# Block-sparse attention with a gated feed-forward block: the band mask by a transposition, block means copied by VectorE, and the scores of the next unit two head pairs at a time

## The chip, the cores and the metric

The kernel runs on one core of one Trainium2 chip. The metric is the device time of one execution in microseconds (us). A core has five engines, each with its own queue, in which instructions stand in order: TensorE (PE) multiplies matrices, VectorE (DVE) and ScalarE (ACT) work on tiles and read the results of PE out of PSUM, GpSimd (POOL) works on tiles and issues DMAs, SyncE (SP) issues DMAs. PSUM has eight banks of 128 x 512 float32 numbers in this kernel: four of the pool `ps_mm`, two of `ps_s`, and one each of `ps_o` and `ps_t`.

## The reference

The first part is attention over 4 batches and 8 heads, with 768 positions and 64 columns a head. Each query sees the keys fewer than 16 positions away, and beside them a summary of every block of 32 positions (the elementwise maximum of its keys, the mean of its values). The second part runs the joined heads through a gated feed-forward block.

```python
k_sum = k.reshape(B, H, nb, block, D).max(axis=3)
v_sum = v.reshape(B, H, nb, block, D).mean(axis=3)
scores_l = scale * np.matmul(q, k.transpose(0, 1, 3, 2))
mask_l = np.abs(pos[:, None] - pos[None, :]) < window
scores_s = scale * np.einsum('bhsd,bhnd->bhsn', q, k_sum) + np.log(block)
scores_l_m = np.where(mask_l, scores_l, -1000000000.0)
a = softmax(np.concatenate([scores_l_m, scores_s], axis=-1))
x = np.matmul(a, np.concatenate([v, v_sum], axis=2))     # heads joined: (3072, 512)
g = x @ w_gate
gelu = 0.5 * g * (1.0 + erf(g / sqrt(2)))
ffn_out = (gelu * (x @ w_val)) @ w_out
out = x + sigmoid(x @ w_res) * ffn_out
```

Here d_ff is 1536 and the model width 512. `softmax` stands for the exponential and the division of the original.

## The kernel before, in words

The work is cut into eight units (`NU`), each half a batch: 384 positions, six tiles of 64 queries, four pairs of heads (`hp`). For a tile of queries, `kW` holds 128 columns of keys: its own 64, 16 on the left and 16 on the right (the rims), 24 block maxima and 8 empty ones. `vext` holds the values in the same order on 128 partitions, the block means on partitions 96 to 127.

A unit goes through these steps:

- **s**, `s_step` and `s_mm`: for a head pair, twelve matmuls of 64 contraction rows (six tiles, two heads) into two banks, one for each head. ScalarE takes the exponential into `P`, and from unit 1 on VectorE multiplies `P` with the band mask `maskt` of zeros and ones (L301). In unit 0 PE adds an additive mask `mneg` of large negative numbers ahead of the scores (L281) and no product is needed.
- **ao**, `av_step`: for a head pair, twelve matmuls of `P` with `vext` into one bank; `av_end` divides by the sum, which is one more column, into `xn` (L339, L341).
- **xT**: `xn` is transposed, in unit 1 by PE and ScalarE (`xt_step`), later by DMAs from SP's queue (`xt_dma`).
- **g, vv**: twelve steps `fo_step`, each with four matmuls for the gate and four for the value; ScalarE takes the Gelu (L366) and VectorE multiplies into `gvT` (L367).
- **r**: `res_step`, four matmuls for each of three blocks of 128 positions (`sub`), and a tanh on ScalarE.
- **f**: `ffn_step`, twelve matmuls for each block into one bank of `ps_mm`; `end_step` works the output out on VectorE (L415, then L418) and SP writes it.

The steps s, ao and xT of unit n + 1 stand within the r and f steps of unit n. The function `first_out` writes out this order for unit 0, `mid_out` for units 1 to 6; unit 7 has `last_out`. The order is that of the code: nothing is scheduled anew (`manual_schedule`), so each engine's queue holds its instructions as they are written. A pool hands its banks out in turn, and whoever gets a bank waits until its last reader is done. `ps_mm` has four banks in turn for g, vv, r, f; `s_step` uses the two banks of `ps_s`; `av_step` uses `ps_o`, or `ps_t` where `other` is given.

Unit 0 starts with loads. GpSimd's queue issues all loads from DRAM, in this order: keys and queries of batch 0, its values, six pairs of pieces of `w_gate` and `w_val` with the second half of the queries (`q_sb[1]`) between them, `w_res`, the rims of the later tiles, `w_out` in three pieces, then keys and values of batch 1. An issue waits for the landing of the eighth load before it. The mask `maskt` is cut out of ones by four selections (L196) after the third pair of pieces. The block means of unit 0 are summed by PE (`vsum_mm`) and copied into `vblk`. Unit 0's own values use `vblk` apart (`av_first`); the tiles 6 to 11 get the means by two copies on GpSimd (`vsum_bc`, L274), behind the issues of `w_out`. `keep_warm` runs matmuls on zeros between steps that wait. The functions `own_keys(bgrp, 3)`, `kw_consts(1)`, `vext_consts(1)` and two memsets of `vsum` fill constants for later batches on VectorE; they stand behind the first two gate steps.

`s_pair` is `s_step` for unit 0 with two banks of `ps_mm` and two exponentials.

Of the kernel before, what the change touches and what calls it, by code (L numbers as in the profile page):

```python
# [15 lines left out]
def kernel(  # L16
# [22 lines left out]
    QT = 64  # L39
# [95 lines left out]
    with tc.manual_schedule():  # L135
# [46 lines left out]
        nc.vector.memset(maskt[:], 1.0)  # L182
# [5 lines left out]
        for c in range(6):  # L188
            sl = slice(c * 256, (c + 1) * 256)
            nc.gpsimd.dma_start(out=w_gate[:, :, sl], in_=wg_src[:, :, sl])  # L190
            nc.gpsimd.dma_start(out=w_val[:, :, sl], in_=wv_src[:, :, sl])  # L191
            if c == 2:
                for lo, hi, sign, base, fill in (
                        (0, QT, 1, WIN - 1, 0.0), (0, QT, -1, WIN - 1, 0.0),
                        (QT, BAND, -1, WIN - 1 - QT, 0.0), (QT, BAND, -1, WIN, 1.0)):
                    nc.gpsimd.affine_select(out=maskt[lo:hi], in_=maskt[lo:hi], compare_op=ALU.is_ge,  # L196
                                            fill=fill, base=base, pattern=[[-sign, QT]],
                                            channel_multiplier=sign)
            if c == 4:
                q_sb[1] = load_q(1, QJ)  # L200
# [92 lines left out]
        def s_step(u, hp, st):  # L293
            s = ps_s.tile([128, 2, 512], F32, tag="s", name="s")
            s_mm(u, hp, [s[:, hh, 0:TU] for hh in range(2)])
            P = ppool.tile([128, 2, HT, QT], BF16, tag="P", name="P")
            nc.scalar.activation(P.rearrange("p a t q -> p a (t q)"), s[:, :, 0:TU], AF.Exp,  # L297
                                 scale=scale, bias=bias_t[:])
# [5 lines left out]
        def s_pair(hp, st):  # L304
            s = [mm_tile("s") for _ in range(2)]
            s_mm(0, hp, [x[:, 0:TU] for x in s])
            P = ppool.tile([128, 2, HT, QT], BF16, tag="P", name="P")
            for hh in range(2):
                nc.scalar.activation(P[:, hh].rearrange("p t q -> p (t q)"), s[hh][:, 0:TU], AF.Exp,
                                     scale=scale, bias=bias_t[:])  # L310
            st["P", hp] = P

# [159 lines left out]
        s_pair(1, st)  # L472
# [6 lines left out]
        s_pair(3, st)  # L479
        vsum_mm(0, vs, 5, 8)  # L480
        keep_warm(2)
        vsum_mm(0, vs, 8, NT)
        keep_warm(2)
# [5 lines left out]
        for i in range(2, 4):  # L489
            vsum_bc(0, 3 * i, 3 * i + 3, nc.gpsimd)  # L490

# [33 lines left out]
        for i in range(2):  # L525
            nc.vector.memset(vsum[i][96:128, :], 0.0)
        own_keys(bgrp, 3)
        kw_consts(1)
        vext_consts(1)


        def first_out(u, st, gvT, nst):
            n = u + 1
            turn = dict(pool=ps_t, tag="t", copy=nc.scalar.copy)
# [24 lines left out]
            xt_step(n, 3, nst, **turn)  # L559
# [124 lines left out]
```

## Time and profile before

| what | us |
|---|---|
| median of 11 runs | 267.07 |
| lowest and highest run | 265.76, 268.00 |
| the profiled execution: its own time | 266.75 |
| its span (first to last instruction) | 265.0 |
| VectorE busy | 154.5 |
| ScalarE busy | 126.2 |
| GpSimd busy | 108.5 |

An engine's busy time is the time in which at least one of its instructions ran. A row of the timeline has the start, the time, the engine, the line, what is written and read, and how many instructions of one kind follow each other; the wait before them stands at its end. A group's row has the busy time and mean nanoseconds of one, then the idle time before and what ended it. A row of windows has, for each engine, its busy time and its instructions, then the granted clock of PE, the mean time of DMA packets and the rate in GB/s. The granted clock was 0.998 of full speed over the whole span.

### The profile page before, as it was taken

The numbers are of one execution on the slowest core, as the hardware profiler recorded it, in microseconds if no ns is written. First come the engines' busy times: TensorE is split into PE (matmuls) and PEld (weight loads), VectorE is DVE, ScalarE is ACT, GpSimd is POOL, SyncE is SP. The second block draws the span as 40 slices with busy tenths as digits, with TensorE's granted clock in tenths as the row PEclk, the third lists the DMA queues.
The fourth block names the chain that finished last, engine by engine and source line by source line (L and its number), as shares of the span: only waits on it lengthen the run. The fifth ranks groups of instructions, "written<-read, shape, count | busy, mean of one in ns | idle before, by whom it ended". The sixth has DMA issues, their size and how long they took to land.

```text
span 265.0 us, 5801 instructions
## 1 busy us (share of the span) xinstructions
PE 257.2 (97%) x2297; PEld 138.2 (52%) x2297; DVE 154.5 (58%) x341; ACT 126.2 (48%) x197; POOL 108.5 (41%) x148
## 2 busy tenths in 40 slices
PE   6999998999999999999999999999999999999993
PEld 2556554545654565445654565445644565456543
DVE  5945732499557544667757444768667544754424
ACT  5774356565382436533373437342473337343320
POOL 8898375293260987253520986252620000000000
PEclk9999999999999999999999999999999999999999
DMA  5999999999743999979903999969803400240002
GB/s 83 175 119 186 197 214 207 188 136 190 72 79 62 171 132 145 103 131 167 134 0 95 161 123 130 121 120 169 131 14 80 127 0 2 46 136 0 0 13 108
DMA packets 98155, 29.61 MB, mean 112 GB/s; under 512 B 83368, under 2 KB 94960, under 8 KB 98016
## 3 DMA queue, kind: packets, MB, share of 16 engines
q0 software_dynamic: 68400, 14.96, 67.0%
q1 hardware_dynamic: 29728, 14.29, 25.0%
q8 instruction: 18, 0.29, 0.5%
q14 instruction: 9, 0.07, 0.1%
HBM read 29.36 MB, written 6.29 MB: 135 GB/s over the span
## 4 chain that ended last, share of the span: by engine, by line
PE 80%; DMA 11%; POOL 5%; DVE 1%; issue 1%; ACT 1%; POOLq 0%
PE f L409 23%; PE g L361 21%; PE vv L361 21%; PE r L399 7%; DMA w_out<-in_moe_w_out_dram 4%; DMA w_gate<-in_moe_w_gate_dram 4%; PE ao L321 3%; PE s L288 3%; DMA q_sb<-in_q_dram 3%; POOL vext L103 1%; POOL w_val L191 1%; POOL w_gate L190 1%; PE f L433 1%; PE vs L262 1%; PE tp L213 1%
## 5 line engine op out<-in xcount | busy, mean ns | idle before, releaser
L367 DVE TENSOR_TENSOR gvT<-ge,vv 128x384 bf16<-128x384 f32 x96 | 52.6, 552 | 53.3 <-PE vv L361 49.0
L366 ACT ACTIVATE ge<-g 128x384 f32<-128x384 f32 x96 | 47.1, 491 | 72.4 <-DVE gvT L367 40.9
L361 PE MATMUL g<-xT,w_gate 128*128 128x384 bf16 x384 | 79.0, 326 | 0.3
L361 PE MATMUL vv<-xT,w_val 128*128 128x384 bf16 x384 | 78.7, 326 | 0.2 <-DVE gvT L367 0.2
L409 PE MATMUL f<-w_out,gvT 128*128 128x512 bf16 x276 | 67.7, 380 | 0.9 <-DMA w_out<-in_moe_w_out_dram 0.9
L361 PEld LDWEIGHTS <-w_val 128*128 128x128 bf16 x384 | 37.5, 98 | 25.4 <-issue 1.0
L361 PEld LDWEIGHTS <-w_gate 128*128 128x128 bf16 x384 | 36.7, 98 | 26.0 <-issue 1.8
L409 PEld LDWEIGHTS <-gvT 128*128 128x128 bf16 x276 | 24.8, 98 | 28.1 <-DMA w_out<-in_moe_w_out_dram 1.4
L103 POOL DMA_DIRECT2D vext<-in_v_dram x48 | 32.9, 724 | 12.1 <-DMA w_out<-in_moe_w_out_dram 4.7
L297 ACT ACTIVATE P<-s,bias_t 128x768 bf16<-128x768 f32 x30 | 27.0, 901 | 15.1 <-PE s L288 14.5
L274 POOL COPY vext<-vsum 32x1536 bf16<-32x1536 bf16 x12 | 17.1, 1464 | 24.1 <-DMA vsum<-vpart 24.1
L415 DVE SCALAR_TENSOR_TENSOR th<-th,f 128x512 f32<-128x512 f32 (+1 forms) x25 | 16.5, 660 | 17.5 <-PE f L409 17.2
L402 ACT ACTIVATE th<-r 128x512 f32<-128x512 f32 x24 | 14.2, 595 | 26.1 <-PE r L399 26.0
L301 DVE TENSOR_TENSOR P<-P,maskt 128x768 bf16<-128x768 bf16 x28 | 15.9, 569 | 18.2 <-ACT P L297 18.2
L399 PE MATMUL r<-w_res,xT 128*128 128x512 bf16 x96 | 24.2, 380 | 0.0
L341 DVE TENSOR_TENSOR xn<-ao,rz 128x384 bf16<-128x384 f32 x32 | 17.8, 557 | 1.1
L418 DVE SCALAR_TENSOR_TENSOR o<-th,xn 128x512 f32<-128x512 f32 (+1 forms) x25 | 16.8, 670 | 0.9
L117 POOL DMA_DIRECT2D k_nat<-in_k_dram x24 | 16.4, 749 | 0.2 <-issue 0.2
L123 POOL DMA_DIRECT2D q_nat<-in_q_dram x18 | 15.9, 918 | 0.7 <-issue 0.6
L220 DVE TENSOR_REDUCE ks<-kW 128x24 bf16<-128x768 bf16 x16 | 15.1, 944 | 0.2
L321 PEld LDWEIGHTS <-P 128*64 128x64 bf16 x336 | 7.5, 110 | 11.9 <-issue 5.9
L399 PEld LDWEIGHTS <-xT 128*128 128x128 bf16 x96 | 8.7, 98 | 9.0
(84 smaller groups left out, 171.2 us busy)
## 6 DMA issues: line engine op xcount, KB each, us to landing
out_dram<-o SPq DMA_DIRECT2D x23, 256.0 KB, 2.2
vext<-in_v_dram POOLq DMA_DIRECT2D x48, 64.0 KB, 6.5
q_nat<-in_q_dram POOLq DMA_DIRECT2D x18, 128.0 KB, 7.3
w_gate<-in_moe_w_gate_dram POOLq DMA_DIRECT2D x6, 256.0 KB, 8.1
w_val<-in_moe_w_val_dram POOLq DMA_DIRECT2D x6, 256.0 KB, 8.7
w_out<-in_moe_w_out_dram POOLq DMA_DIRECT2D x3, 512.0 KB, 11.8
k_nat<-in_k_dram POOLq DMA_DIRECT2D x24, 64.0 KB, 4.7
vext<-vext SPq DMA_DIRECT2D x6, 144.0 KB, 5.4
```

Of the source, the lines that this page charges most:

```text
L103: nc.gpsimd.dma_start(out=vext[b % 2][0:QT, t, :, 0:D], in_=v[b, :, t * QT:(t + 1) * QT, :].rearrange("h p d -> p h d"))
L117: nc.gpsimd.dma_start(out=k_nat[:, t].rearrange("p (h d) -> p h d", d=D), in_=k[b, :, t * QT:(t + 1) * QT, :].rearrange("h p d -> p h d"))
L274: eng.tensor_copy(vext[b % 2][96:128, lo:hi, :, 0:D], src)
L297: nc.scalar.activation(P.rearrange("p a t q -> p a (t q)"), s[:, :, 0:TU], AF.Exp, scale=scale, bias=bias_t[:])
L341: nc.vector.tensor_mul(xn, ao[:, :, :, 0:D], rz.to_broadcast([128, NSUB, 2, D]))
L361: nc.tensor.matmul(ps[:, 0:TU], w[:, ko, fo * 128:(fo + 1) * 128], st["xT"][:, ko, :], start=(ko == 0), stop=(ko == KO - 1), skip_group_ch ...
L366: nc.scalar.activation(ge[:], g[:, 0:TU], AF.Gelu)
L367: nc.vector.tensor_mul(gvT[:, fo, :], ge[:], vv[:, 0:TU])
L399: nc.tensor.matmul(r[:], st["xT"][:, ko, ss], w_res[:, ko, :], start=(ko == 0), stop=(ko == KO - 1))
L409: nc.tensor.matmul(st["f", sub][:], gvT[:, fo, ss], w_out[:, fo, :], start=(fo == 0), stop=(fo == FO - 1), skip_group_check=True)
L415: nc.vector.scalar_tensor_tensor(th[:, cs], th[:, cs], 1.0, f[:, 0:n], ALU.add, ALU.mult)
L418: nc.vector.scalar_tensor_tensor(o.rearrange("p (k d) -> p k d", d=128), th[:, cs].rearrange("p (k d) -> p k d", d=128), 0.5, x, ALU.mult, ...
```

## The change

There are five edits.

- In units 1 to 6 (`mid_out`) scores 0 and 1 stand together, value products 0 and 1 with scores 2 and 3 behind them, and value products 2 and 3 together. Scores 1 lie in the banks of `ps_t` and `ps_o` (`TO2`), scores 3 in two banks of `ps_mm` (`MM2`); both have two exponentials of 384 columns. The blocks of r and f move between them.
- In unit 0 (`first_out`) scores 0 and 1 stand together, and value products 0 and 1. The last transposition (`xt_step` 3) stands ahead of the last four f.
- The mask `maskt` is no longer selected by GpSimd from ones. PE transposes `mneg` into a bank, and VectorE compares it with -1. This stands in `unit0_extras`, behind gate step 2.
- The block means for tiles 6 to 11 are copied by VectorE, two tiles behind each of the gate steps 4 to 6. The constants for later batches are spread over steps 2 to 9.
- In unit 0 the sums of values (`vsum_mm`) run through without the four warming matmuls between and behind them, and the products with own values follow them.

```diff
-        nc.vector.memset(maskt[:], 1.0)
...
-            if c == 2:
-                for lo, hi, sign, base, fill in (
...
-                    nc.gpsimd.affine_select(out=maskt[lo:hi], in_=maskt[lo:hi], compare_op=ALU.is_ge,
...
-        def s_step(u, hp, st):
-            s = ps_s.tile([128, 2, 512], F32, tag="s", name="s")
-            s_mm(u, hp, [s[:, hh, 0:TU] for hh in range(2)])
+        def s_step(u, hp, st, banks=None):
+            if banks:
+                s = [p.tile([128, 512], F32, tag=tag, name="s") for p, tag in banks]
+            else:
+                s2 = ps_s.tile([128, 2, 512], F32, tag="s", name="s")
+                s = [s2[:, hh] for hh in range(2)]
+            s_mm(u, hp, [x[:, 0:TU] for x in s])
...
+            if banks:
+                for hh in range(2):
+                    nc.scalar.activation(P[:, hh].rearrange("p t q -> p (t q)"), s[hh][:, 0:TU], AF.Exp,
+                                         scale=scale, bias=bias_t[:])
...
+        MM2 = ((ps_mm, "mm"),) * 2
+        TO2 = ((ps_t, "t"), (ps_o, "ao"))
...
-        vsum_mm(0, vs, 5, 8)
-        keep_warm(2)
-        vsum_mm(0, vs, 8, NT)
-        keep_warm(2)
+        vsum_mm(0, vs, 5, NT)
...
-        for i in range(2, 4):
-            vsum_bc(0, 3 * i, 3 * i + 3, nc.gpsimd)
...
+        def unit0_extras(fo):
+            if fo == 2:
+                mt = ps_o.tile([128, 128], BF16, tag="ao", name="mt")
+                nc.tensor.transpose(mt[:], mneg[:], ident[:])
+                nc.vector.tensor_scalar(out=maskt[:], in0=mt[:, 0:QT], scalar1=-1.0, scalar2=None,
+                                        op0=ALU.is_ge)
+                own_keys(bgrp, 3)
+            elif fo == 3:
+                kw_consts(1)
+            elif fo < 7:
+                vsum_bc(0, 2 * fo - 2, 2 * fo, nc.vector)
+            elif fo == 7:
+                vext_consts(1)
+            elif fo < 10:
+                nc.vector.memset(vsum[fo - 8][96:128, :], 0.0)
 
         def first_out(u, st, gvT, nst):
...
             s_step(n, 0, nst)
+            s_step(n, 1, nst, TO2)
             res_step(st, 0)
             res_step(st, 1)
             ffn_step(st, gvT, 0, 0, 4)
+            av_step(n, 0, nst)
+            av_step(n, 1, nst, **other)
+            s_step(n, 2, nst)
             ffn_step(st, gvT, 1, 0, 4)
-            av_step(n, 0, nst)
-            s_step(n, 1, nst)
             res_step(st, 2)
             ffn_step(st, gvT, 2, 0, 4)
-            ffn_step(st, gvT, 0, 4, 8)
-            av_step(n, 1, nst)
-            s_step(n, 2, nst)
             xt_step(n, 0, nst, **turn)
-            ffn_step(st, gvT, 1, 4, 8)
-            ffn_step(st, gvT, 2, 4, 8)
             av_step(n, 2, nst)
             s_step(n, 3, nst)
+            ffn_step(st, gvT, 0, 4, 8)
+            ffn_step(st, gvT, 1, 4, 8)
             xt_step(n, 1, nst, **turn)
+            ffn_step(st, gvT, 2, 4, 8)
+            av_step(n, 3, nst)
+            xt_step(n, 2, nst, **turn)
             ffn_step(st, gvT, 0, 8, FO)
             end_step(u, st, 0)
             ffn_step(st, gvT, 1, 8, FO)
-            av_step(n, 3, nst)
-            xt_step(n, 2, nst, **turn)
+            xt_step(n, 3, nst, **turn)
             ffn_step(st, gvT, 2, 8, FO)
-            xt_step(n, 3, nst, **turn)
             end_step(u, st, 1)
             end_step(u, st, 2)
...
             s_step(n, 0, nst)
+            s_step(n, 1, nst, TO2)
             res_step(st, 0)
-            ffn_step(st, gvT, 0, 0, 2)
-            s_step(n, 1, nst)
-            ffn_step(st, gvT, 0, 2, 6)
+            res_step(st, 1)
+            ffn_step(st, gvT, 0, 0, 4)
             av_step(n, 0, nst)
             xt_dma(0, nst)
-            s_step(n, 2, nst)
-            ffn_step(st, gvT, 0, 6, 11)
             av_step(n, 1, nst, **other)
             xt_dma(1, nst)
-            s_step(n, 3, nst)
-            ffn_step(st, gvT, 0, 11, FO)
-            res_step(st, 1)
+            s_step(n, 2, nst)
+            s_step(n, 3, nst, MM2)
+            ffn_step(st, gvT, 0, 4, FO)
+            ffn_step(st, gvT, 1, 0, 3)
             av_step(n, 2, nst)
             xt_dma(2, nst)
-            ffn_step(st, gvT, 1, 0, 4)
             av_step(n, 3, nst, **other)
             xt_dma(3, nst)
             end_step(u, st, 0)
-            ffn_step(st, gvT, 1, 4, FO)
+            ffn_step(st, gvT, 1, 3, FO)
             res_step(st, 2)
             end_step(u, st, 1)
             ffn_step(st, gvT, 2, 0, FO)
```

How the queues change is shown at three places; behind the line stand the operation, what it writes and reads, and its shape. On VectorE, these are the rows of unit 1's output phase before, from the mask products of head pairs 0 and 1 to the first step of `end_step`:

```order
L301 TENSOR_TENSOR P<-P,maskt 128x768 x2
L339 RECIPROCAL rz<-ao 128x6
L341 TENSOR_TENSOR xn<-ao,rz 128x384
L301 TENSOR_TENSOR P<-P,maskt 128x768
L339 RECIPROCAL rz<-ao 128x6
L341 TENSOR_TENSOR xn<-ao,rz 128x384
L301 TENSOR_TENSOR P<-P,maskt 128x768
L339 RECIPROCAL rz<-ao 128x6
```

And these are the same rows now:

```order
L302 TENSOR_TENSOR P<-P,maskt 128x768 x2
L334 RECIPROCAL rz<-ao 128x6
L336 TENSOR_TENSOR xn<-ao,rz 128x384
L334 RECIPROCAL rz<-ao 128x6
L336 TENSOR_TENSOR xn<-ao,rz 128x384
L302 TENSOR_TENSOR P<-P,maskt 128x768 x2
L334 RECIPROCAL rz<-ao 128x6
```

The mask products of pairs 2 and 3 stood behind the division of pair 0 and of pair 1; now both stand behind that of pair 1. On ScalarE, the same phase before, from the last Gelu to the load of the table for the next:

```order
L366 ACTIVATE ge<-g 128x384 x12
L297 ACT_TABLE_LOAD
L297 ACTIVATE P<-s,bias_t 128x768
L402 ACTIVATE th<-r 128x512
L297 ACTIVATE P<-s,bias_t 128x768 x3
L402 ACTIVATE th<-r 128x512 x2
L366 ACT_TABLE_LOAD
```

And now:

```order
L361 ACTIVATE ge<-g 128x384 x12
L298 ACT_TABLE_LOAD
L298 ACTIVATE P<-s,bias_t 128x768
L295 ACTIVATE P<-s,bias_t 128x384 x2
L397 ACTIVATE th<-r 128x512 x2
L298 ACTIVATE P<-s,bias_t 128x768
L295 ACTIVATE P<-s,bias_t 128x384 x2
L397 ACTIVATE th<-r 128x512
L361 ACT_TABLE_LOAD
```

Two of the four wide exponentials are now two narrow ones each, and two tanh stand between the pairs. On GpSimd, the loads of the start before, from the last piece ahead of the mask:

```order
L191 DMA w_val<-in_moe_w_val_dram 128x4x256
L196 AFFINE_SELECT maskt<-maskt 64x64 x2
L196 AFFINE_SELECT maskt<-maskt 32x64 x2
L190 DMA w_gate<-in_moe_w_gate_dram 128x4x256
L191 DMA w_val<-in_moe_w_val_dram 128x4x256
```

And now:

```order
L190 DMA w_val<-in_moe_w_val_dram 128x4x256
L189 DMA w_gate<-in_moe_w_gate_dram 128x4x256
L190 DMA w_val<-in_moe_w_val_dram 128x4x256
L189 DMA w_gate<-in_moe_w_gate_dram 128x4x256
L190 DMA w_val<-in_moe_w_val_dram 128x4x256
```

The selections are gone, and the loads keep their order.

More of the change, by code (lines that the diff above doesn't have):

```diff
@@ L302, in s_step @@
             st["P", hp] = P
[L304 to L311, printed above, removed]
+        MM2 = ((ps_mm, "mm"),) * 2
+        TO2 = ((ps_t, "t"), (ps_o, "ao"))
         def av_step(u, hp, st, pool=ps_o, tag="ao"):
@@ L524 @@
         gv_end(gvT, 1, g1, v1)
[L525 to L529, printed above, removed]
+        def unit0_extras(fo):
[13 more added lines that the diff above has]
+                nc.vector.memset(vsum[fo - 8][96:128, :], 0.0)
         def first_out(u, st, gvT, nst):
             n = u + 1
+            other = dict(pool=ps_t, tag="t")
             turn = dict(pool=ps_t, tag="t", copy=nc.scalar.copy)
             s_step(n, 0, nst)
+            s_step(n, 1, nst, TO2)
             res_step(st, 0)
@@ L619 @@
                     fo_step(st, gvT, fo)
+                if u == 0:
+                    unit0_extras(fo)
                 if u == 0 and fo >= 8:
```

13 lines of the change are left out of this document (5 added, 8 removed).

## The prediction

> **What bounds the kernel now.** I read the share of each engine on the page first, then the chain that ended last, then TensorE's own waits, and only then its timeline in one unit.
>
> ```profile
> PE 257.2 (97%) x2297; PEld 138.2 (52%) x2297; DVE 154.5 (58%) x341; ACT 126.2 (48%) x197; POOL 108.5 (41%) x148
> ```
> ```profile
> PE 80%; DMA 11%; POOL 5%; DVE 1%; issue 1%; ACT 1%; POOLq 0%
> ```
> ```profile
> PE xp L346 <- DVE xn L341: 0.2, 1, 0.2
> ```
>
> TensorE (PE) is 97% busy and carries 80% of the chain. The third row is the whole answer of the waits of PE between 56 and 248 us: once, for 0.2 us. So in units 1 to 6 nothing holds PE up from outside, and time can only leave there if PE's own stream gets shorter. A busy share of 97% does not say that the stream is as short as it can be, since the page counts the end of each matmul, which is pipelined, as busy. The places where the starts stand further apart than the work needs must be looked for in the timeline. This is unit 1's output phase, with one row per run of equal matmuls:
>
> ```profile
> 75.11 0.35 PE L288 MATMUL s<-qT,kW 64*128 64x64 bf16 x12
> 75.39 1.04 PE L399 MATMUL r<-w_res,xT 128*128 128x512 bf16 x4
> ```
> ```profile
> 77.07 1.04 PE L409 MATMUL f<-w_out,gvT 128*128 128x512 bf16 x4
> 78.04 0.38 PE L321 MATMUL ao<-vext,P 128*64 128x65 bf16 x12
> 78.35 0.35 PE L288 MATMUL s<-qT,kW 64*128 64x64 bf16 x12
> 78.63 1.25 PE L409 MATMUL f<-w_out,gvT 128*128 128x512 bf16 x5
> ```
> ```profile
> 85.78 2.75 PE L409 MATMUL f<-w_out,gvT 128*128 128x512 bf16 x12
> 88.37 0.65 PE L361 MATMUL g<-xT,w_gate 128*128 128x384 bf16 x3
> ```
>
> Starts count here. Twelve f from 85.78 to 88.37 take 2.59, or 0.216 each, so the four f from 77.07 need 0.86, but the value product (ao) starts 0.97 later: **0.10 us lost on the way into it**. For the way out I asked for narrow windows, in which the last two matmuls of a group stand alone:
>
> ```profile
> 75.26 0.19 PE L288 MATMUL s<-qT,kW 64*128 64x64 bf16 x2
> ```
>
> The score group (s) starts at 75.11 and its sixth pair at 75.26, so a pair takes 0.03. The residual product r follows at 75.39, 0.13 after that pair: **again 0.10 lost**. So a group of twelve costs 0.18 us of work and 0.10 wherever the shape of the tile in the third last column (64*128, 128*64, 128*128) changes.
>
> The other bound lies at the front. Up to 43.88 us the chain is not PE's:
>
> ```profile
> 32.67 11.16 DMA w_out<-in_moe_w_out_dram
> ```
> ```profile
> 43.88 1.90 PE L409 MATMUL f<-w_out,gvT 128*128 128x512 bf16 x8 [0.90 <-DMA w_out<-in_moe_w_out_dram]
> ```
>
> The first third of w_out is issued at 32.67 and lands 11.16 us later, at 43.83; PE, which stood still for 0.90 us, starts f on it.
>
> **Part 1: the order of unit 1 to 6's output phase.** Counted in the code's order, the old phase changes shape 14 times: into s, s to r, f to s, s to f, f to ao, ao to s, s to f, the last three once more, then r to ao, ao to f, f to ao, ao to f. The new one (scores 0 and 1 together, value products 0 and 1 with scores 2 and 3 behind them, value products 2 and 3 together) changes 7 times. The number of s, ao, r and f matmuls is the same. Seven changes at 0.10 are 0.70 us a unit.
>
> What two joined groups cost is shown for value products by one row only, and for scores by none:
>
> ```profile
> 16.89 0.61 PE L441 MATMUL wp<-warm 128*128 128x512 bf16 x2
> 17.43 1.04 PE L254 MATMUL vs<-vext,bmat 64*32 64x256 bf16 x8
> 18.40 0.60 PE L441 MATMUL wp<-warm 128*128 128x512 bf16 x2
> 18.94 0.95 PE L333 MATMUL ao<-vext,P 96*64 96x65 bf16 x48
> ```
>
> Four groups of twelve in a run keep PE busy for 0.95 here, 0.24 each against 0.31 from start to start for a single one. The join of two scores may cost from 0 to 0.10 on each side, thus 0.30 to 0.70 saved a unit. I take 0.70, because the pairs inside a group already follow each other at 0.03. The Trainium skill, "TensorEngine Tiling (Array Packing)", Tiling Modes, says that a change of the tiling mode drains the engine, and a change of the tile alone does not. By that rule joins are free and the saving is 0.70; without it, by the entries alone, it would be 0.30.
>
> What can now be late. Scores 1 and 3 lie in two separate banks, so ScalarE takes two exponentials of 384 columns instead of one of 768:
>
> ```profile
> 75.72 0.90 ACT L297 ACTIVATE P<-s,bias_t 128x768 bf16<-128x768 f32 x1
> 76.52 0.59 ACT L402 ACTIVATE th<-r 128x512 f32<-128x512 f32 x1
> ```
> ```profile
> 13.97 1.07 ACT L309 ACTIVATE P<-s,bias_t 128x384 bf16<-128x384 f32 x2
> ```
>
> The next instruction follows a wide one after 0.80; the pair takes 1.07; VectorE's mask product takes 0.57:
>
> ```profile
> L301 DVE TENSOR_TENSOR P<-P,maskt 128x768 bf16<-128x768 bf16 x28 | 15.9, 569 | 18.2 <-ACT P L297 18.2
> ```
>
> So in the new order exponential 0 runs at 75.72 and the two of pair 1 until 77.6. The first value product needs the bank that the second of them frees. On PE it comes after two scores (0.46 with the exit), 12 matmuls of r and f (2.59) and an entry (0.10), at 75.11 + 3.15 = 78.26: 0.66 in hand. The mask product of pair 1 ends near 78.2, and pair 1 is wanted at 78.45. Scores 2 start near 78.76, and exponentials 2 and 3 end near 81.2, the mask product of 3 near 81.8; it is wanted at 81.9. These waits I cost at nothing: the r and f matmuls hide them, but with only 0.1 to 0.7 to spare.
>
> One wait I do expect. Four banks turn over in the order r0, r1, f0, the two of score 3, f1, r2, f2: r2 now takes f0's bank, where it took r0's before. f0's bank is free when VectorE's first step of `end_step` (L415) has read it, and that step stands behind the last value product's division:
>
> ```profile
> 82.87 0.38 PE L321 MATMUL ao<-vext,P 128*64 128x65 bf16 x12
> ```
> ```profile
> 83.36 0.20 DVE L339 RECIPROCAL rz<-ao 128x6 f32<-128x6 f32 x1 [0.56 <-PE ao L321]
> 83.59 0.56 DVE L341 TENSOR_TENSOR xn<-ao,rz 128x384 bf16<-128x384 f32 x1
> 84.07 0.68 DVE L415 SCALAR_TENSOR_TENSOR th<-th,f 128x512 f32<-128x512 f32 x1
> ```
>
> New order on PE: the third value product at 81.69 (78.26, plus 0.51 for two joined products, 0.46 for two scores, eleven f at 0.216, one entry). VectorE's division starts 0.49 behind it (82.87 to 83.36 in the old unit), takes 0.71 up to the next and 0.71 again, so L415 runs from 83.60 to 84.28. PE reaches r2 after another 0.51 and nine f, at 84.15. **A new wait of about 0.18 a unit**, from 0 (VectorE a little earlier) to 0.45 (later by half a step). f2, queued behind r2, and the next unit wait with it. Sum: 6 x (0.70 - 0.18) = **3.1 us**, between 6 x 0.25 = 1.5 and 6 x 0.70 = 4.2. The transposing DMAs of xT are issued at about the same time as before (the last value product's division ends near 83.7 against 84.1) and are wanted by the next unit 4 us later.
>
> **Part 2: the output phase of unit 0.** From 43.88 on it does the same with 11 changes, now 8, and score 1 moves ahead of w_out's landing, into time in which PE waits anyway. Its end had two waits:
>
> ```profile
> 55.86 0.34 PE L346 MATMUL xp<-ident,xn 128*128 128x128 bf16 x3 [0.16 <-DVE xn L341]
> 56.04 1.05 PE L361 MATMUL g<-xT,w_gate 128*128 128x384 bf16 x4
> 56.93 0.81 PE L361 MATMUL vv<-xT,w_val 128*128 128x384 bf16 x4
> ```
>
> 0.16 before the last transposition, and 0.24 inside the first gate product (0.89 from start to start against 0.65 elsewhere), which needs that transposition's copy. In the new order four f stand behind it (0.86) and hide the copy. Gain: three changes 0.30, score 1 0.18, the waits 0.40: **0.9 us**. Without the joins it is 0.6. The old order wants the second third of w_out some 4 us after the first and does not wait for it; the new one wants it more than 5 us after.
>
> **Part 3: unit 0 ahead of 43.88.** Four warming matmuls go: 16.89 to 17.43 and 18.40 to 18.94, 1.08 us. The mask transposition adds one matmul, some 0.06 (three take 0.18). VectorE gets the mask comparison, the old memsets spread over eight steps, and three copies of 32 partitions with 1024 elements; GpSimd loses two copies and the four selections of the mask (shown below).
>
> ```profile
> 14.80 1.03 DVE L475 COPY vext<-vext 16x3072 bf16<-16x3072 bf16 x1
> ```
> ```profile
> 36.28 2.87 POOL L274 COPY vext<-vblk 32x1536 bf16<-32x1536 bf16 x2
> ```
>
> A VectorE copy of 1024 elements lies between a third of the 1.03 and the whole of it; I take 0.4. I cost all of Part 3 at **nothing**, for an earlier PE then meets data that have not landed:
>
> ```profile
> PEld L246 <- DMA q_sb<-in_q_dram: 0.3, 1, 0.3
> ```
> ```profile
> 35.41 0.36 PE L246 MATMUL tp<-ident,q_sb 96*64 96x96 bf16 x8
> ```
>
> It already waits for the second half of q, near 35.4. Arriving 1 us earlier it waits 1 us longer, and once more for w_out until 43.83. What would count is an earlier landing, and the DMA rings decide that:
>
> ```profile
> 16.50:19.00 2.50, 2.50 (x21) 1.11 (x20) 0.43 (x1) 1.26 (x4) 2.50 (x4) 1.00 1.25 165
> 19.00:20.50 1.50, 1.50 (x72) 1.23 (x73) 0.00 (x0) 1.38 (x2) 1.31 (x6) 1.00 1.09 85
> 20.50:44.00 23.50, 22.16 (x203) 12.54 (x196) 11.80 (x42) 12.15 (x24) 15.39 (x20) 1.00 1.37 203
> ```
>
> From 20.5 to 44 us they move a steady 203 GB/s, and GpSimd issues w_out only when an earlier load has landed. Earlier issue does not help a full queue.
>
> **Sum.** 266.75 (the profiled execution: span 265.0 and 1.75 around it) - 3.1 - 0.9 = 262.75. The median of the runs shown, 267.07, lies 0.3 higher, so I forecast **263.0**.
>
> **Rivals.**
> A faster front. In the second row above the rings drop to 85 GB/s for 1.5 us, just when GpSimd makes the mask:
>
> ```profile
> 19.06 1.17 POOL L196 TENSOR_SCALAR_AFFINE_SELECT maskt<-maskt 64x64 bf16<-64x64 bf16 x4
> ```
>
> If that work holds up the loads, w_out lands up to 1.5 x (1 - 85/203) = 0.9 earlier, and everything with it: 262.1. Against it stands the load issued just ahead:
>
> ```profile
> w_val<-in_moe_w_val_dram POOLq DMA_DIRECT2D x1, 256.0 KB, 8.6
> ```
>
> It takes 8.6 us to landing, so the queue was full of earlier loads throughout. Chance 0.15.
>
> Entries only. If a joined group still loses its exit, 0.30 a unit remains; PE then reaches r2 after L415 and does not wait there: 6 x 0.30 + 0.6 = 2.4, or 264.7. Chance 0.14.
>
> Slower. r2's bank wait grows: every 0.1 us that VectorE's L415 comes later is 0.6 us in all. To be slower than before by 0.2% (what a measurement of this kernel can tell from no change) it must come 0.75 us a unit later than worked out, about a mask product plus a division late. Six waits of 0.93 instead of 0.18 give 267.6. For it: mask products 2 and 3 now stand right ahead of the two divisions. Against it: VectorE has no more work than before, and is busy for 58% of the span. Chance 0.07.
>
> VectorE's copies hold up GpSimd's issue of w_out. Next to such copies one issue took 1.01 instead of 0.75:
>
> ```profile
> 14.06 1.01 POOL L190 DMA_DIRECT2D w_gate<-in_moe_w_gate_dram  x1
> ```
> ```profile
> 13.69 1.07 DVE L474 COPY vext<-vext 32x2560 bf16<-32x2560 bf16 x1
> ```
>
> Three copies at 0.3 make 0.9 if nothing hides them: 263.9. The 11 us that a w_out load stands in the queue should. The Trainium skill, "SBUF — State Buffer", SBUF: two separate sides, says that a VectorE copy in a two-port mode locks GpSimd out so that it cannot write descriptors; the row agrees. Chance 0.03.
>
> **How the numbers follow.** The forecast has 0.58, between 261.9 and 264.3 by the bounds of the r2 wait; the faster front 0.15, entries only 0.14, slower 0.07, the held issue 0.03, and 0.03 that the waits eat everything. The range is 261.2 to 265.2: it takes in the first rivals on both sides. Faster 0.90, within 0.2% 0.03, slower 0.07.
>
> **What would show it.** Two joined scores at 0.36 and two joined value products at 0.41 from first start to last pair's end; 12.6 to 12.9 us from the first score to the next gate product in units 1 to 6 instead of 13.26; a wait of r on VectorE's L415 step of 0.1 to 0.3, six times; a wait of about 1 us for q_sb near 35, and f again at 43.8 to 43.9. A landing of w_out before 43.3 would make Part 3 wrong, and waits of the value products for exponentials would make Part 1's cover wrong.

## The result, and the profile after

| | median us | runs | lowest to highest |
|---|---|---|---|
| before | 266.95 | 31 | 265.76 to 268.0 |
| after | 261.43 | 8 | 260.89 to 261.97 |

The ratio of after to before is 0.9793, with a 95% interval from 0.9778 to 0.9809: the changed kernel is faster by 5.5 us. The forecast was 263.0, within 261.2 to 265.2; the time lies inside the range, near its lower end, and 0.5 below the 261.9 to which the forecast's own case reached. The profiled execution took 261.45 us with a span of 259.5.

Line numbers have moved: s is now L280, r L394, f L404, ao L316, the narrow exponentials L295 and the wide ones L298, the mask product L302, the division L334 and L336, `end_step` L410 and L413. The shares on the page, to set beside the first row of the prediction:

```profile
PE 251.2 (97%) x2294; PEld 137.9 (53%) x2294; DVE 155.3 (60%) x344; ACT 126.5 (49%) x210; POOL 104.6 (40%) x142
```

The share of PE is 97% as before, though 6.0 us of its busy time are gone. The waits of PE over the whole span (total us, times, longest):

```profile
PE wp L436 <- DVE warm L156: 1.2, 1, 1.2
PE tp L238 <- DMA q_sb<-in_q_dram: 1.2, 1, 1.2
PE tp L205 <- DMA k_sb<-in_k_dram: 0.9, 1, 0.9
PE f L404 <- DMA w_out<-in_moe_w_out_dram: 0.5, 1, 0.5
PE s L280 <- ACT qT L240: 0.3, 1, 0.3
```

All of them lie in unit 0's start, and none is a wait of r for `end_step`. To see where 5.5 us went, I cut both spans at two events: the first f, which w_out's landing releases, and the first value matmul (vv) of unit 1. The windows from one to the other and from there to the end, before:

```profile
43.88:56.93 13.05, 12.80 (x140) 6.34 (x141) 7.36 (x16) 5.89 (x11) 5.60 (x9) 1.00 1.47 166
56.93:265.00 208.07, 204.13 (x1693) 109.97 (x1691) 122.15 (x238) 94.11 (x146) 69.64 (x86) 1.00 0.81 97
```

And after:

```profile
44.10:56.05 11.95, 11.95 (x128) 6.26 (x128) 6.83 (x16) 6.50 (x11) 4.82 (x8) 1.00 1.48 168
56.05:259.50 203.45, 199.51 (x1694) 109.87 (x1691) 121.77 (x238) 93.47 (x158) 70.34 (x87) 1.00 0.84 100
```

The second column is the length of the stretch. Up to the first f the changed kernel is 0.22 us later. From there to unit 1 it is **1.10 shorter** (Part 2 of the prediction), and from there to the end **4.62 shorter** (Part 1). The sum is 5.5. In the last stretch ScalarE has 12 instructions more (158, two a unit) and PE the same work, at a granted clock of 1.00 in both. How the 4.62 are spread, from the windows that hold one output phase each, from the first score to the next gate product. Before, unit 1:

```profile
75.11:88.37 13.26, 13.26 (x145) 6.27 (x145) 8.67 (x18) 7.16 (x9) 3.87 (x6) 1.00 0.28 74
```

After, unit 1:

```profile
74.23:86.72 12.49, 12.49 (x145) 6.27 (x145) 8.49 (x18) 7.14 (x11) 2.80 (x4) 1.00 0.25 64
```

The same 145 matmuls take 12.49 instead of 13.26, and the other five units repeat it within 0.01: 6 x 0.77 = 4.62. PE counts as busy throughout in both, so the busy share cannot show this gain. The timeline of PE in unit 1's phase does:

```profile
74.23 0.52 PE L280 MATMUL s<-qT,kW 64*128 64x64 bf16 x24
74.68 1.90 PE L394 MATMUL r<-w_res,xT 128*128 128x512 bf16 x8
76.42 1.03 PE L404 MATMUL f<-w_out,gvT 128*128 128x512 bf16 x4
77.38 0.57 PE L316 MATMUL ao<-vext,P 128*64 128x65 bf16 x24
77.88 0.52 PE L280 MATMUL s<-qT,kW 64*128 64x64 bf16 x24
78.34 2.55 PE L404 MATMUL f<-w_out,gvT 128*128 128x512 bf16 x11
80.81 0.57 PE L316 MATMUL ao<-vext,P 128*64 128x65 bf16 x24
81.31 2.12 PE L404 MATMUL f<-w_out,gvT 128*128 128x512 bf16 x9
83.27 1.03 PE L394 MATMUL r<-w_res,xT 128*128 128x512 bf16 x4
84.13 2.75 PE L404 MATMUL f<-w_out,gvT 128*128 128x512 bf16 x12
```

Twenty-four scores take 0.45 from their start to that of r, where twelve took 0.28: the second twelve cost 0.17 and no change of shape. Now the last three rows beside VectorE's timeline at the same place, with the first step of `end_step`:

```profile
82.63 0.68 DVE L410 SCALAR_TENSOR_TENSOR th<-th,f 128x512 f32<-128x512 f32 x1
```

The third block of r starts at 83.27, while L410 still reads f0's bank until 83.31. The prediction had r wait for the end of L410. A distance of 0.04 is too small to decide that by itself, so the fourth experiment moves the two apart.

### The profile page after: what moved, and what is told of

It is laid out like the page before. It is cut to its first block, busy times and chain, and to the rows that moved or that the text cites. A ratio compares the mean times of both kernels' runs of the same rounds, so it can differ in the third digit from the quotient of the medians.

```text
span 259.5 us, 5798 instructions
## 1 busy us (share of the span) xinstructions
PE 251.2 (97%) x2294; PEld 137.9 (53%) x2294; DVE 155.3 (60%) x344; ACT 126.5 (49%) x210; POOL 104.6 (40%) x142
## 4 chain that ended last, share of the span: by engine, by line
PE 81%; DMA 12%; POOL 4%; issue 1%; DVE 0%; POOLq 0%
PE f L404 24%; PE g L356 21%; PE vv L356 21%; PE r L394 8%; DMA w_out<-in_moe_w_out_dram 5%; DMA w_gate<-in_moe_w_gate_dram 4%; DMA q_sb<-in_q_dram 3%; PE ao L316 3%; PE s L280 2%; POOL vext L103 1%; POOL w_val L190 1%; POOL w_gate L189 1%; PE f L428 1%; PE vs L254 1%; PE tp L205 1%; POOL k_sb L88 1%
## 5 line engine op out<-in xcount | busy, mean ns | idle before, releaser
L404 PE MATMUL f<-w_out,gvT 128*128 128x512 bf16 x276 | 64.9, 380 | 0.5 <-DMA w_out<-in_moe_w_out_dram 0.5
L404 PEld LDWEIGHTS <-gvT 128*128 128x128 bf16 x276 | 25.7, 98 | 29.9 <-issue 0.8
L103 POOL DMA_DIRECT2D vext<-in_v_dram x48 | 32.7, 727 | 12.6 <-DMA w_out<-in_moe_w_out_dram 4.7
L397 ACT ACTIVATE th<-r 128x512 f32<-128x512 f32 x24 | 13.6, 605 | 28.4 <-PE r L394 28.4
L410 DVE SCALAR_TENSOR_TENSOR th<-th,f 128x512 f32<-128x512 f32 (+1 forms) x25 | 16.5, 661 | 15.8 <-PE f L404 15.5
L302 DVE TENSOR_TENSOR P<-P,maskt 128x768 bf16<-128x768 bf16 x28 | 15.9, 569 | 12.4 <-ACT P L298 7.7
L394 PE MATMUL r<-w_res,xT 128*128 128x512 bf16 x96 | 23.2, 380 | 0.0
L336 DVE TENSOR_TENSOR xn<-ao,rz 128x384 bf16<-128x384 f32 x32 | 17.8, 557 | 1.1
L413 DVE SCALAR_TENSOR_TENSOR o<-th,xn 128x512 f32<-128x512 f32 (+1 forms) x25 | 17.2, 687 | 0.9
L298 ACT ACTIVATE P<-s,bias_t 128x768 bf16<-128x768 f32 x17 | 15.3, 901 | 4.8 <-PE s L280 4.6
L295 ACT ACTIVATE P<-s,bias_t 128x384 bf16<-128x384 f32 x30 | 15.7, 578 | 0.3 <-PE s L280 0.3
L394 PEld LDWEIGHTS <-xT 128*128 128x128 bf16 x96 | 8.8, 98 | 9.9
```

What stands on the lines that cost most here:

```text
L103: nc.gpsimd.dma_start(out=vext[b % 2][0:QT, t, :, 0:D], in_=v[b, :, t * QT:(t + 1) * QT, :].rearrange("h p d -> p h d"))
L336: nc.vector.tensor_mul(xn, ao[:, :, :, 0:D], rz.to_broadcast([128, NSUB, 2, D]))
L394: nc.tensor.matmul(r[:], st["xT"][:, ko, ss], w_res[:, ko, :], start=(ko == 0), stop=(ko == KO - 1))
L404: nc.tensor.matmul(st["f", sub][:], gvT[:, fo, ss], w_out[:, fo, :], start=(fo == 0), stop=(fo == FO - 1), skip_group_check=True)
L410: nc.vector.scalar_tensor_tensor(th[:, cs], th[:, cs], 1.0, f[:, 0:n], ALU.add, ALU.mult)
L413: nc.vector.scalar_tensor_tensor(o.rearrange("p (k d) -> p k d", d=128), th[:, cs].rearrange("p (k d) -> p k d", d=128), 0.5, x, ALU.mult, ...
```

## The experiments

Each kernel is the changed one with one edit (e10 has two); each was timed in turn with the kernel before on the same chip. There the kernel before had medians of 267.03 (e1 to e4), 267.07 (e5 to e8) and 266.53 (b1, e9, e10), so between these groups the ratios are to be compared and not the medians. The single spans have a scatter of their own, which is why this table has the parts beside them. "Landing" is that of the first third of w_out, "unit 0" the stretch from the first f to unit 1's first vv, and "phase" the output phase of units 1 to 6, the same in all six within 0.01; all are of the profiled execution.

| kernel | median us | ratio to before, 95% interval | landing | unit 0 | phase | span |
|---|---|---|---|---|---|---|
| before | 266.95 | 1 | 43.84 | 13.05 | 13.26 | 265.0 |
| after | 261.43 | 0.9793 [0.9778, 0.9809] | 44.06 | 11.95 | 12.49 | 259.5 |
| e1_mid_old | 265.45 | 0.995 [0.9926, 0.9974] | 43.51 | 11.95 | 13.26 | 263.6 |
| e2_first_old | 262.23 | 0.9837 [0.9805, 0.9868] | 43.79 | 13.05 | 12.49 | 260.4 |
| e3_front_old | 261.53 | 0.9803 [0.9779, 0.9826] | 44.03 | 11.96 | 12.49 | 259.5 |
| e4_split5 | 260.93 | 0.9784 [0.9756, 0.9811] | 43.56 | 11.95 | 12.49 | 259.0 |
| e5_scores_apart | 262.64 | 0.9849 [0.9808, 0.989] | 43.05 | 11.95 | 12.74 | 260.0 |
| e6_products_apart | 262.51 | 0.9843 [0.98, 0.9886] | 44.13 | 11.95 | 12.72 | 261.0 |
| e7_dummy64 | 260.92 | 0.9778 [0.9743, 0.9814] | 43.04 | 11.96 | 12.52 | 258.7 |
| e8_dummy128 | 262.2 | 0.9827 [0.9794, 0.9861] | 43.43 | 11.97 | 12.74 | 260.4 |
| b1_changed_again | 260.97 | 0.979 [0.9771, 0.9808] | 43.72 | 11.95 | 12.49 | 259.2 |
| e9_res2_first | 259.97 | 0.9761 [0.9736, 0.9786] | 43.12 | 11.10 | 12.49 | 257.8 |
| e10_res2_q_later | 260.69 | 0.9777 [0.9759, 0.9796] | 43.83 | 11.09 | 12.49 | 258.8 |

### Each part alone

The first three kernels put one part of the change back.

The old order of units 1 to 6, with the rest as changed:

```diff
-        def mid_out(...):   # order of the changed kernel
+        def mid_out(...):   # order of the kernel before, with its 14 changes of shape
```

> The changed kernel with the output phase of units 1 to 6 in its old order, all else as changed. Theory (the gain is made of changes of tile shape on TensorE, 7 fewer in each of six phases, 0.77 us a phase in the trace): 4.6 us slower than the changed kernel, near 266.0, and 13.26 us from the first score to the next gate product, as in the kernel before. Rival (a good part of the gain comes from unit 0, through earlier loads): less than 3.5 us slower, under 265.

The phase is 13.26 again in all six units, and unit 0 stays at 11.95. The stretch from unit 1's first vv to the end is back too:

```profile
43.55:55.50 11.95, 11.95 (x128) 6.26 (x128) 6.83 (x16) 6.50 (x11) 3.49 (x6) 1.00 1.41 165
55.50:263.60 208.10, 204.13 (x1694) 109.98 (x1691) 122.81 (x238) 93.62 (x146) 71.69 (x89) 1.00 0.83 98
```

208.10 against 203.45: 4.6 us hang on `mid_out` alone. The median moved by 4.0 only; in the profiled execution w_out landed 0.55 earlier than in that of the changed kernel, and the rest followed it.

The old order of unit 0's output phase:

```diff
-        def first_out(...):   # order of the changed kernel
+        def first_out(...):   # order of the kernel before
```

> The changed kernel with the output phase of unit 0 in its old order. Theory (this phase gives 0.9 to 1.1 us, of which some is the wait for the last transposition at its end): 262.3 to 262.6, and the wait of the first gate product of unit 1 is back with 0.2 to 0.4 us. Rival (the phase only waits for w_out, and its order counts for nothing): 261.4.

The stretch behind the first f is 13.05 as before, 1.10 longer. These are the rows of its PE timeline at the end of unit 0's phase:

```profile
54.63 1.03 PE L404 MATMUL f<-w_out,gvT 128*128 128x512 bf16 x4
55.82 0.34 PE L341 MATMUL xp<-ident,xn 128*128 128x128 bf16 x3 [0.17 <-DVE xn L336]
56.00 1.05 PE L356 MATMUL g<-xT,w_gate 128*128 128x384 bf16 x4
```

The idle time before the last transposition is 0.17. From the start of the four f to it, however, there are 1.19, where four f take 0.86 when nothing is waited for (the twelve f from 84.13 to the gate product at 86.72 in the changed kernel's unit 1 are 0.216 each). So the wait cost 0.33, twice what its bracket says: the idle time begins only at the modelled end of the last matmul, and the first half of the wait lies under that end.

The old start of unit 0 (the mask by GpSimd's selections, the block means of tiles 6 to 11 by GpSimd, the constants behind gate step 1, the four warming matmuls), with both new orders:

```diff
+        nc.vector.memset(maskt[:], 1.0)
+            if c == 2:
+                for lo, hi, sign, base, fill in (
...
-        vsum_mm(0, vs, 5, NT)
+        vsum_mm(0, vs, 5, 8)
+        keep_warm(2)
+        vsum_mm(0, vs, 8, NT)
+        keep_warm(2)
...
+        for i in range(2, 4):
+            vsum_bc(0, 3 * i, 3 * i + 3, nc.gpsimd)
...
-                if u == 0:
-                    unit0_extras(fo)
```

> The changed kernel with the old start of unit 0: mask selected by GpSimd, block means copied by GpSimd, the four warming matmuls and the constants where they were; the output phases are the new ones. Theory (TensorE meets loads that have not landed whatever it saves there): the same time as the changed kernel within 0.3 us, 261.1 to 261.8, with the first f starting at 43.8 to 44.2. Rival (the start gives part of the gain): 0.9 us slower or more, over 262.3.

The ratio is 0.9803 against 0.9793, inside each other's interval, and the span 259.5 in both. PE no longer waits for `q_sb`, whose transpositions start at 35.46 here and at 35.29 in the changed kernel; w_out lands at 44.03 here and at 44.06 there. So the other three of the five edits move no time that this comparison can tell, as Part 3 said: what PE gains at the start it spends in front of the landings. A small gain is not excluded, however. The interval of e3 alone is 0.6 us wide to each side, and e4 below, timed beside e3 with the new start and with the same stretches behind the first f, has a median of 260.93, 0.6 lower, and its w_out landed 0.47 earlier. In the eleven kernels with the new start w_out was issued at 31.16 to 32.24, in the two with the old one at 32.55 and 32.67; the landings of the two groups overlap (43.04 to 44.13, and 43.84 and 44.03). Whether the start is worth nothing or some half a microsecond stays open.

### The wait that did not come

Five f matmuls of block 1 instead of three stand ahead of value products 2 and 3, and seven instead of nine behind them. The last division and with it L410 then come later against r, which keeps its place in the phase:

```diff
-            ffn_step(st, gvT, 1, 0, 3)
+            ffn_step(st, gvT, 1, 0, 5)
...
-            ffn_step(st, gvT, 1, 3, FO)
+            ffn_step(st, gvT, 1, 5, FO)
```

> The changed kernel with five f of block 1 instead of three ahead of value products 2 and 3, so that these and VectorE's steps behind them come 0.43 us later while r of block 2 is reached at the same time. Theory A (that r waits for VectorE's first step of end_step on f0, and has no slack left): a wait of TensorE on VectorE of 0.3 to 0.45 us in each of six phases, 1.8 to 2.7 us slower, 263.2 to 264.1. Theory B (r does not depend on that step, which is why the forecast wait did not come): the same time, 261.4, and no wait.

The PE timeline of unit 1's phase, at its end:

```profile
80.75 0.57 PE L316 MATMUL ao<-vext,P 128*64 128x65 bf16 x24
81.25 1.69 PE L404 MATMUL f<-w_out,gvT 128*128 128x512 bf16 x7
82.77 1.03 PE L394 MATMUL r<-w_res,xT 128*128 128x512 bf16 x4
```

And VectorE's:

```profile
82.57 0.68 DVE L410 SCALAR_TENSOR_TENSOR th<-th,f 128x512 f32<-128x512 f32 x1
```

r starts at 82.77, 0.48 before L410 ends, without a wait, and the phase stays at 12.49. **r does not depend on this step of `end_step`.** In the program as built, the third block of r does not lie in f0's bank: the pool gave it the bank of the first half of score 3, which that score's exponential frees some 3 us earlier (its two narrow exponentials, in the changed kernel):

```profile
79.07 1.04 ACT L295 ACTIVATE P<-s,bias_t 128x384 bf16<-128x384 f32 x2
```

They end at 80.11. f0's bank is taken again only in the next unit. The pool picked the bank that the code before had released first. The banks did not turn over in order, as the description of the kernel and the prediction had it.

### The price of one change of shape

Two kernels take one join apart each, with two changes of shape more a unit. The scores, with the first block of r between them:

```diff
             s_step(n, 0, nst)
-            s_step(n, 1, nst, TO2)
             res_step(st, 0)
+            s_step(n, 1, nst, TO2)
```

> The changed kernel with r of block 0 put between scores 0 and 1 in units 1 to 6; the same matmuls otherwise. It adds two changes of tile shape a phase. Theory (a change costs about 0.10 us on each side of a group, and a join saves both): the phase grows from 12.49 to 12.70 us, the kernel by 1.2 us to 262.6. Rival 1 (a join saves the entry only): 12.59 and 262.0. Rival 2 (the gain comes from where r and f stand, not from the joins): 12.49 and 261.4. A wait of a value product for its exponential would show as a wait of TensorE and is not part of either.

The value products, with one f between them:

```diff
             av_step(n, 0, nst)
             xt_dma(0, nst)
+            ffn_step(st, gvT, 0, 4, 5)
             av_step(n, 1, nst, **other)
...
-            ffn_step(st, gvT, 0, 4, FO)
+            ffn_step(st, gvT, 0, 5, FO)
```

> The changed kernel with one f put between value products 0 and 1 in units 1 to 6; the same matmuls otherwise. Two more changes of tile shape a phase. Theory (0.10 us on each side): the phase is 12.69 to 12.71 us instead of 12.49, the kernel 1.2 us slower, 262.6. Rival 1 (a join saves the entry only): 12.59 and 262.0. Rival 2: no difference.

PE waits for nothing behind 52 us in either, and the phase is 12.74 in the first and 12.72 in the second: 0.25 and 0.23 more for two changes. In e6's timeline of unit 1 both can be seen:

```profile
77.45 0.38 PE L316 MATMUL ao<-vext,P 128*64 128x65 bf16 x12
77.77 0.39 PE L404 MATMUL f<-w_out,gvT 128*128 128x512 bf16 x1
78.08 0.38 PE L316 MATMUL ao<-vext,P 128*64 128x65 bf16 x12
78.40 0.52 PE L280 MATMUL s<-qT,kW 64*128 64x64 bf16 x24
```

The single f takes 0.31 from start to start, and 0.216 in a run: the change back to ao costs 0.10. The change into f is in the 0.32 of the first product.

These two move real work about. The next two leave all work where it is and put one matmul on zeros between scores 0 and 1; it writes columns of score 0's bank that nobody reads. One has the scores' shape, the other 128 rows:

```diff
             s_mm(u, hp, [x[:, 0:TU] for x in s])
+            if u > 1 and hp == 0:
+                nc.tensor.matmul(s2[:, 0, 384:448], warm[0:64, 0:128], warm[0:64, 0:64], start=True, stop=True,
+                                 skip_group_check=True)
```

with `warm[0:128, ...]` in both operands of the second.

> The changed kernel with one more matmul on zeros behind score 0 of units 2 to 7, in the tile shape of the scores (64 rows, 128 columns, 64 numbers in each row); its result is not used. Theory (what costs is the change of the tile shape): 0.03 to 0.06 us in each of six phases, 12.52 to 12.55 us. Rival (any foreign matmul between two groups costs an entry and an exit): 12.7 us.

> The same as the run with the matmul of 64 rows, but that matmul has 128 rows and so the shape of the large products, with the same 64 numbers in each row. Theory (what costs is the change of the tile shape): two changes more, 12.70 to 12.76 us a phase, 0.18 to 0.22 more than with 64 rows, 1.2 us in all. Rival (any foreign matmul costs the same): no difference between 64 and 128 rows.

The timelines of unit 1, in which the lines behind the edit stand three further down, first of the 64-row one:

```profile
73.22 0.35 PE L280 MATMUL s<-qT,kW 64*128 64x64 bf16 x12
73.41 0.19 PE L293 MATMUL s<-warm 64*128 64x64 bf16 x1
73.41 0.36 PE L280 MATMUL s<-qT,kW 64*128 64x64 bf16 x12
73.70 1.90 PE L397 MATMUL r<-w_res,xT 128*128 128x512 bf16 x8
```

Then of the 128-row one:

```profile
73.62 0.35 PE L280 MATMUL s<-qT,kW 64*128 64x64 bf16 x12
73.90 0.20 PE L293 MATMUL s<-warm 128*128 128x64 bf16 x1
74.04 0.35 PE L280 MATMUL s<-qT,kW 64*128 64x64 bf16 x12
74.32 1.90 PE L397 MATMUL r<-w_res,xT 128*128 128x512 bf16 x8
```

Up to r, 24 scores and the matmul take 0.48 with 64 rows and 0.70 with 128. The phase is 12.52 against 12.74, the stretch from unit 1's vv to the end 203.65 against 204.94. The difference is 1.29 / 6 = 0.215 a unit, for two changes. So one change costs 0.11 here too, and a matmul of the same shape 0.03. The Trainium skill, "TensorEngine Tiling (Array Packing)", Tiling Modes, says that a change of mode drains the engine; these two rows agree, and they price one change at 0.11 us in this kernel.

### A version that is faster still

In unit 0 PE waits for w_out with the third block of r still to be done. The edit moves that block ahead of the first f, into the wait:

```diff
             res_step(st, 1)
+            res_step(st, 2)
             ffn_step(st, gvT, 0, 0, 4)
...
-            res_step(st, 2)
```

> The changed kernel with r of block 2 moved ahead of the first f in unit 0, into the time in which TensorE waits for w_out. Theory (0.4 to 0.5 us of that wait lie on the path that sets the end, and 0.86 us of work fill it): 0.4 to 0.5 us faster than the changed kernel, 260.9 to 261.0, with no wait for w_out left and the first f at 44.1 to 44.4. Rival (what stands behind then waits instead, for a bank or an exponential): 261.4.

It is the fastest kernel here: 259.97 us, a ratio of 0.9761 [0.9736, 0.9786] to before, with 0.979 [0.9771, 0.9808] for the changed kernel timed again beside it on the same chip (b1_changed_again, whose expectation follows).

> The changed kernel once more, beside the next two on the same chip: 261.4 us, every theory alike.

The intervals of the two overlap a little; the stretch in the profile does not depend on the landing and is plain. Rows of PE's timeline around the wait in b1:

```profile
41.20 1.90 PE L394 MATMUL r<-w_res,xT 128*128 128x512 bf16 x7
43.76 1.02 PE L404 MATMUL f<-w_out,gvT 128*128 128x512 bf16 x4 [0.66 <-DMA w_out<-in_moe_w_out_dram]
```

And in e9, from a window that begins within r:

```profile
40.98 2.32 PE L394 MATMUL r<-w_res,xT 128*128 128x512 bf16 x10
43.17 1.04 PE L404 MATMUL f<-w_out,gvT 128*128 128x512 bf16 x4
```

In e9 r runs up to the first f without a wait, and f starts 0.05 after w_out's landing (43.12). From the first f to unit 1 it takes 11.10 instead of 11.95, the whole 0.85 of the block of r. I had expected about half, because I had taken the bracket for the size of the hole. It is the point of e2 once more: eight r from 41.20 (one is missing in the row's count) leave PE free at 41.20 + 8 x 0.216 = 42.93, and f starts at 43.76, so the hole was 0.83 wide and not 0.66. The other 0.60 between the two spans is w_out's landing, which came that much earlier in e9's profiled execution (43.12 against 43.72). That the block fitted so well is in part the luck of this execution: its twelve r, from 40.54, end at 43.13, just as w_out lands. In the first profile of the changed kernel the hole was 44.10 - 41.67 - 8 x 0.216 = 0.70, and the block of 0.86 would have pushed f back by 0.16.

The last kernel adds to e9 that the transpositions of the second half of q stand one gate step later, behind their landing:

```diff
-                if u == 0 and fo >= 8:
-                    q_step(1, fo - 8, ps_t, "t")
+                if u == 0 and fo >= 9:
+                    q_step(1, fo - 9 if fo < 11 else 3, ps_t, "t")
+                    if fo == 10:
+                        q_step(1, 2, ps_o, "ao")
```

> As the run before, and the transpositions of the second half of q one gate step later each, so that TensorE works on gate step 9 while it waits for q now (1.2 us). Theory (w_out's landing bounds the start of the first f, and TensorE is held by w_val's last pieces meanwhile): 0 to 0.3 us faster than the run before, 260.6 to 261.0; the wait for q is gone, a wait for w_gate and w_val of 0.5 to 1.2 us takes its place. Rival (the wait for q is on the path): 1 us faster than the run before.

The wait for `q_sb` is gone, and others stand in its place. PE's waits from 25 to 56 us:

```profile
PE vv L356 <- ACT ge L361: 0.5, 1, 0.5
PE g L356 <- DMA w_gate<-in_moe_w_gate_dram: 0.4, 1, 0.4
...
PE vv L356 <- DMA w_val<-in_moe_w_val_dram: 0.2, 1, 0.2
```

PE runs into the next pieces of the weights, waits 0.2 and 0.4 for them, and 0.5 for the Gelu of the late gate product. f then starts 0.35 after the landing instead of 0.05. At 260.69 it is no gain over e9, where 0 to 0.3 had been expected: the loads set the pace there.

## Why the prediction came out as it did

**What bounds the kernel: right.** PE's own stream bounds units 1 to 6 and the landing of w_out the start. Behind 52 us PE has no wait in the changed kernel, and in each of the 13 profiles f starts within 0.05 of the landing (0.35 in e10, where PE is late).

**Part 1, the changes of shape: right, a little too small.** Seven changes at 0.10 were to give 0.70 a unit. They gave 0.77, or 0.11 each, and e5, e6 and e8 against e7 find 0.11 to 0.13 apart from the change itself. Joins are free: the rival "entries only" (264.7) falls, since 24 scores need only 0.17 more than 12, and 24 value products 0.19 more (0.50 against 0.31).

**Part 1, the wait of r2: wrong, and the one step that failed.** The prediction took 0.18 off each unit since r2 would take f0's bank and wait for VectorE (its own times leave 0.13, from 84.15 to 84.28). Its times were nearly exact: from the phase's first score it put the first value product at +3.15, the third at +6.58, L410 from +8.49 to +9.17, and r2 behind that wait at +9.04 plus 0.18. The trace has +3.15, +6.58, L410 from +8.40 to +9.08, and r2 at +9.04. What was wrong was who waits for whom, which e4 shows: with L410 ending 0.48 after r2's start nothing is lost. The four banks do not turn over in order, and r2 has the bank of score 3. So the phase is 12.49, below the 12.6 to 12.9 that the prediction named. Without this term the prediction's own sum would have been 266.75 - 4.2 - 0.9 = 261.65. The slower rival (six waits of 0.93) falls with it, as it grew from the same dependency. That 261.43 still lies inside the range is luck in part: the forecast's own case ended at 261.9 even with no wait at all (this sum and the 0.3 up to the median of before), and the range went down to 261.2 to take in the rival of a faster front, which the runs do not show. (The case's upper bound of 264.3 lacks the 0.3 that its lower one has: 266.75 - 1.5 - 0.9 + 0.3 is 264.6.)

**Part 1, the cover: right.** No value product waited for an exponential or a mask product. The narrow exponentials of pair 1 ended at +2.44 (76.67), where +2.49 was worked out, and the VectorE products of pairs 0 and 1 at +3.04.

**Part 2: right, 1.10 instead of 0.9.** Three changes are 0.33 and score 1 is 0.17. The mis-sized term is the wait for the last transposition: costed at the 0.16 in its bracket, it was worth 0.33, because the modelled end of the f before covers half of it. With 0.24 inside the first gate product the sum is 1.07. No run takes these four terms apart.

**Part 3: right as far as the runs can tell.** e3, with all of the old start back, is not told from the changed kernel, while e4 beside it leaves room for half a microsecond. The copies on VectorE took 0.43 each, as estimated, between multiplications into `gvT` that wait for PE anyway:

```profile
30.81 0.43 DVE L266 COPY vext<-vblk 32x1024 bf16<-32x1024 bf16 x1
31.61 0.56 DVE L362 TENSOR_TENSOR gvT<-ge,vv 128x384 bf16<-128x384 f32 x1 [0.37 <-PE vv L356]
```

The wait for `q_sb` grew to 1.17, where about 1 was forecast, and f started at 44.10 rather than 43.8 to 43.9.

**The rivals at the start.** The faster front supposed that the rings dropped to 85 GB/s because GpSimd made the mask. Without any selection the same window of the changed kernel reads:

```profile
19.00:20.50 1.50, 1.50 (x54) 1.10 (x49) 1.18 (x4) 0.61 (x2) 1.50 (x3) 1.00 1.17 107
```

And in e3, where the four selections run from 19.15 to 20.32, it reads:

```profile
19.00:20.50 1.50, 1.50 (x68) 1.23 (x69) 0.00 (x0) 1.44 (x2) 1.31 (x6) 1.00 1.06 127
```

The rate is 107 GB/s without the selections and 127 with them, so the dip does not come from them, and in the changed kernel's profile w_out landed no earlier. The held issue falls as well: in the chain of the changed kernel w_out is issued a little earlier than before (32.24 against 32.67), and lands later only because it takes longer.

```profile
32.24 11.82 DMA w_out<-in_moe_w_out_dram
```

Next to VectorE's third copy that issue took 0.77 in the changed kernel, 0.86 in b1 and 0.91 in e9, and the issue behind it 0.76 in all three, so a copy held it up by 0.15 at most.

So nearly all of the 1.30 us between the prediction's sum (262.75) and the profiled execution (261.45) can be named: 6 x 0.18 for a wait that did not exist, 6 x 0.07 and 0.2 for the two sizes, less 0.22 for a later landing and 0.20 for more time around the span (1.95 against 1.75). That makes 1.28. Of the 0.27 by which the forecast was off beyond that, 0.25 was what it added to reach the median of before.

## What to carry to other kernels

When matmuls of different tile shapes alternate on TensorE, count the changes of shape and price one from start-to-start distances; the busy share shows nothing of it. Before a new wait on a PSUM bank is put into a sum, look up in the built program which bank the tile really gets, since two engines' times that meet within 0.1 us prove no dependency. The hole that a wait leaves on TensorE is the distance between starts less the work, and not the idle time of the row.

## What the runs showed of the hardware beyond that

The landing of the first third of w_out scatters by 1.1 us between profiled executions (43.04 to 44.13), also among kernels that are alike up to that point (e5 43.05, e6 44.13), and everything behind it shifts with it, so that two single spans of this kernel can't be compared below 1 us. The stretches behind the landing repeat within 0.03 us between kernels whose code is the same there. And the price of a change of shape was nearly the same for a group of real work and for one matmul on zeros: 0.11 to 0.13 us, taken as half of what two changes cost.
